# One written order for block 0, with scores set directly ahead of the preceding unit's outputs

## The chip, the core and the metric

The kernel runs on one core of a Trainium2 chip. The metric is the device time in microseconds (us) of one execution; the time of a kernel is the median over its runs. TensorE (PE) multiplies matrices into PSUM; VectorE (DVE), ScalarE (ACT) and GpSimd (POOL) do elementwise work; SyncE (SP) issues nearly all loads here. Each engine works through its own list of instructions in order and waits on semaphores for the others.

## What is computed

A linear-attention recurrence (RWKV) over 4 batches, 8 heads and 768 tokens of 48 channels, and after it a feed-forward layer on the 3072 tokens of 384 channels. The feed-forward weights come as 64-bit floats.

```python
for t in range(S):                                   # attention, per batch b and head h
    cur = einsum('bhd,bhe->bhde', u * k[:, :, t], v[:, :, t])
    y[:, :, t] = einsum('bhd,bhde->bhe', r[:, :, t], state + cur)
    state = w * state + einsum('bhd,bhe->bhde', k[:, :, t], v[:, :, t])
x = y.transpose(0, 2, 1, 3).reshape(B * S, H * D)    # 3072 x 384
h = x @ w_in                                         # 384 x 2048
g = where(h > 0, h, exp(min(h, 0)) - 1)
out = g @ w_out                                      # 2048 x 384
```

## The kernel before

The 768 tokens are cut into 6 blocks of 128. A **unit** is one block of one batch, written n.b: unit 1.2 is block 1 of batch 2. A block has 4 units, that is 512 tokens, and its feed-forward layer runs in 16 steps f, one for each 128 of the 2048 hidden channels.

**A unit's work.** `turn_in` (T) transposes r and k on TensorE; `decay_r` and `decay_k` (dr, dk, line L688) multiply them on VectorE by powers of w and their inverses; `scores` (A, L768) multiplies the two into two PSUM banks of scores; `take_scores` (pa, pb, L849) copies the scores under the mask over a diagonal that `diag_scores` wrote (Dp, Dq on GpSimd, Ep, Eq on ScalarE); `outputs` (Y) adds the state's part (`by_state`, L807 and L812), the scores' part (`by_keys`, L824) and, in the same call, makes the unit's contribution to the next state (`added_state`, L924); `split_x` (xh, xl) writes the result as a high and a low fp32r part; `new_state` (ns) updates the state; `key_rest` (kr, krd; L740) scales k for the state ahead of that. In block 0 there is no old state: `mask_scores` (m0, m1), `current_by_v` (vd, L859) and `first_outputs` (Y, L880 and L824) stand there, and S is `new_state`.

**A step of the layer.** `hidden` (hid f, L1031) is 9 matmuls of 512 columns, `project` (proj f, L1083) 9 more; between them stand `negative` (neg: two ScalarE passes, L1040 and L1041), `elu` (L1046, VectorE), and `split_g` (gh on ScalarE L1052, gl on VectorE L1054). `hidden` writes one of only two PSUM buffers named h, so hid f+2 can begin only when gl f has read the one of hid f.

**Weights.** They come once, during block 0, as pieces j: j = 2f is w_in's part f, j = 2f+1 is w_out's. Lw:j is the load (L212, L215). `widen` (wd, ScalarE L571), `merge` (ma, VectorE L580), `split_w` (sp; ScalarE L593 for w_in, GpSimd L591 for w_out) and `rest_w` (rs, rsd; VectorE L617, GpSimd or VectorE L615) make of a pair of 64-bit pieces two fp32r tables wh and wl, which stay in SBUF. The layer in block 0 therefore runs while its own weights are still coming.

**What sets the order.** Every engine gets its instructions in the order in which the program calls the helpers. Before block 0's layer that is the string START: words `name:unit`, called by `do`. Then comes BOTH for steps 0 to 2, and from step 3 on `step(n, f)` goes through the words of FIRST, the same ones at every step of block 0; a word such as A1 acts at the step that is one behind a unit's begin, and the units of block 1 begin at steps 2, 5, 8 and 11 (`BEGIN`). Blocks 1 to 5 go through LATER in the same manner. There, from unit 2.1 on, `insertion` (word AY) puts the scores of one unit directly ahead of the outputs of the unit before it: scores cut into 32-column pieces (L792) and then L807, L812, L824, L924, with one of the h buffers taken as an output buffer. In block 0 scores (L768) and outputs of block 1's units stand apart, each between matmuls of the layer.

Of the kernel before, what the change touches and what calls it, by code (L numbers as in the profile page):

```python
# [19 lines left out]
P = 128  # L20
# [16 lines left out]
EARLY = (0, 6)  # L37
# [16 lines left out]
proj krd1 swd2 Dp0 r3 rudx rudA-2 sumA-1 wd third tT+0
# [5 lines left out]
BEGIN = [2, 5, 8, 11]  # L60
# [6 lines left out]
class Kernel:  # L67
# [241 lines left out]
    def start(self):  # L309
# [3 lines left out]
        for b in (2, 3):  # L313
# [33 lines left out]
            "m1a": lambda b: self.mask_scores(0, b, 1, True),  # L347
            "vd": lambda b: self.current_by_v(0, b),
# [34 lines left out]
    def first_steps(self):  # L383
# [782 lines left out]
```

## Time and profile before

| | |
|---|---|
| median of 3 runs | 497.28 us (496.21 to 499.79) |
| the profiled execution | 496.31 us, its span 494.6 us |
| TensorE busy in the span | 485.3 us (98%) |
| VectorE, ScalarE, GpSimd busy | 304.2, 240.7, 107.3 us |
| busy from 25 to 110 us (block 0's layer): TensorE, VectorE, ScalarE | 84.09, 76.08, 58.15 of 85 us |
| loads | 49.11 MB in all; 184 GB/s over the first 25 us |

The span is from the first to the last instruction that the profile records; the rest of an execution lies around it. "Idle" of an engine is time between its instructions; a row gives it in brackets with the engine that ended it. Matmul rows overlap, so the cost of a group on TensorE is read here from starts: the start of the first matmul behind the group, less that of the last one ahead of it.

### The profile page before, as it was taken

Reading aid. Unit: us, or ns where it says so; the run is one execution under the profiler, and the core shown is the slowest. Engines: PE = TensorE matmul, PEld = TensorE weight load, DVE = VectorE, ACT = ScalarE, POOL = GpSimd, SP = SyncE. Lnnn points to the kernel's source line nnn. Section 1 sums busy time; section 2 is a strip of 40 time slices with the busy share of each in tenths; the row PEclk is TensorE's granted clock in tenths of the full one; section 3 lists DMA queues with packets and bytes.
Section 4 is the critical chain, followed back from the end, with each engine's and each line's share of the span. In section 5 each row is a group of like instructions: output and inputs, shape, how many; then the busy total and the mean of one; then the engine's idle time right before and its main releaser. Section 6 shows DMA issues by size and latency. Waiting matters only on the chain.

```text
span 494.6 us, 12125 instructions
## 1 busy us (share of the span) xinstructions
PE 485.3 (98%) x5013; PEld 403.4 (82%) x5013; DVE 304.2 (61%) x533; ACT 240.7 (49%) x458; POOL 107.3 (22%) x142
## 2 busy tenths in 40 slices
PE   8999999999999999999999999999999999999995
PEld 7787778787888888888888888888888888889995
DVE  7899988884686557657556575574674343433332
ACT  4377766734454444535435435445354453344341
POOL 7623332441132331221321321301011000000000
PEclk9999999999999999999999999999999999999999
DMA  9899987483364652544513625514343000010001
GB/s 142 223 231 204 213 197 190 94 153 89 84 139 105 135 121 43 130 118 72 121 52 84 151 67 108 142 44 92 101 79 100 11 1 2 8 33 20 5 0 69
DMA packets 108453, 49.11 MB, mean 99 GB/s; under 512 B 89442, under 2 KB 104292, under 8 KB 108388
## 3 DMA queue, kind: packets, MB, share of 16 engines
q1 hardware_dynamic: 96292, 43.52, 40.0%
q10 hardware_dynamic: 12096, 4.72, 4.0%
q8 instruction: 41, 0.67, 0.6%
q14 instruction: 24, 0.20, 0.1%
HBM read 35.12 MB, written 13.11 MB: 98 GB/s over the span
## 4 chain that ended last, share of the span: by engine, by line
PE 93%; DMA 3%; SPq 2%; DVE 1%; issue 0%; ACT 0%; DVEq 0%
PE ps_acc L1083 40%; PE ps_h L1031 39%; PE ps_y L824 4%; PE ps_a L792 4%; PE ps_y L812 1%; PE ps_y L924 1%; PE ps_a L768 1%; PE ps_y L807 1%; DMA raw<-in_k_dram 1%; DMA stage<-in_moe_w_out_dram 1%; DMA r_t<-in_r_dram 1%; SPq L169 1%; PE ps_y L880 1%; SPq L165 1%; PE ps_kT L628 0%; DMA w_col<-in_w_dram 0%
## 5 line engine op out<-in xcount | busy, mean ns | idle before, releaser
L1031 PE MATMUL ps_h<-x,wh 128*128 128x512 f32 (+1 forms) x582 | 192.6, 388 | 0.0
L1083 PE MATMUL ps_acc<-g,wh 128*128 128x512 f32 x480 | 164.6, 397 | 0.1
L1046 DVE SCALAR_TENSOR_TENSOR ps_h<-g,ps_h 128x512 f32<-128x512 f32 x96 | 66.6, 694 | 123.8 <-ACT g L1041 123.6
L1031 PEld LDWEIGHTS ps_h<-x,wh 128*128 128x128 f32 x582 | 108.8, 188 | 23.0 <-DVE g L1054 0.5
L1040 ACT ACTIVATE g<-ps_h 128x512 f32<-128x512 f32 x96 | 57.3, 596 | 123.2 <-PE ps_h L1031 95.0
L1031 PE MATMUL ps_h<-x,wl 128*128 128x512 f32 (+1 forms) x291 | 112.7, 387 | 0.0
L1083 PEld LDWEIGHTS ps_acc<-g,wh 128*128 128x128 f32 x480 | 90.0, 188 | 21.2 <-issue 0.8
L1054 DVE SCALAR_TENSOR_TENSOR g<-ps_h,g 128x512 fp32r<-128x512 f32 x96 | 66.3, 690 | 45.3 <-ACT g L1052 40.4
L1083 PE MATMUL ps_acc<-g,wl 128*128 128x512 f32 x240 | 93.6, 390 | 0.0
L1052 ACT ACTIVATE g<-ps_h 128x512 fp32r<-128x512 f32 x96 | 57.4, 598 | 72.7 <-DVE ps_h L1046 62.7
L1031 PEld LDWEIGHTS ps_h<-x,wl 128*128 128x128 f32 x291 | 54.7, 188 | 10.9
L1041 ACT ACTIVATE g<-g 128x512 f32<-128x512 f32 x96 | 60.7, 632 | 3.1
L842 POOL TENSOR_TENSOR a<-ident,diag 128x512 f32<-128x512 f32 x20 | 20.9, 1044 | 149.9 <-PE ps_y L924 81.2
L1083 PEld LDWEIGHTS ps_acc<-g,wl 128*128 128x128 f32 x240 | 45.1, 188 | 8.5
L676 POOL TENSOR_TENSOR tb<-rk,qw 128x512 f32<-128x512 f32 x16 | 20.7, 1297 | 70.3 <-DMA rk<-blocks 61.2
L1083 PE MATMUL ps_acc<-wh,g 128*128 128x384 f32 x128 | 33.8, 335 | 0.0
L849 DVE COPY_PREDICATED a<-mask,ps_a 128x512 f32<-128x512 int32 x40 | 29.3, 732 | 0.0
L838 ACT ACTIVATE a<-ident,diag 128x128 f32<-128x128 f32 x80 | 25.3, 391 | 0.0
L1083 PEld LDWEIGHTS ps_acc<-wh,g 128*128 128x128 f32 x128 | 23.2, 188 | 0.3
L571 ACT ACTIVATE wide<-stage 128x768 f16<-128x768 bf16 (+1 forms) x18 | 17.8, 991 | 9.9 <-DMA stage<-in_moe_w_in_dram 8.7
L949 ACT CAST x<-ps_y 128x256 fp32r<-128x256 f32 (+1 forms) x40 | 10.8, 324 | 22.8 <-DVE state L939 21.4
L1083 PE MATMUL ps_acc<-wl,g 128*128 128x384 f32 x64 | 21.4, 335 | 0.0
(114 smaller groups left out, 440.2 us busy)
## 6 DMA issues: line engine op xcount, KB each, us to landing
blocks<-tb SPq DMA_DIRECT2D x64, 128.0 KB, 2.3
rk<-blocks SPq DMA_DIRECT2D x16, 512.0 KB, 3.4
stage<-in_moe_w_out_dram SPq DMA_DIRECT2D x16, 383.8 KB, 5.4
stage<-in_moe_w_in_dram SPq DMA_DIRECT2D x64, 95.8 KB, 4.3
out_dram<-stage ACTq DMA_DIRECT2D x80, 48.0 KB, 1.7
r_t<-in_r_dram SPq DMA_DIRECT2D x17, 192.0 KB, 4.3
k_t<-in_k_dram SPq DMA_DIRECT2D x17, 192.0 KB, 4.9
v_t<-in_v_dram SPq DMA_DIRECT2D x17, 192.0 KB, 5.3
```

What stands on the lines that cost most here:

```text
L676: (self.nc.gpsimd if i else self.nc.vector).tensor_mul(dst, src, by)
L792: nc.tensor.matmul(un["pa"][i][keys, a * P : (a + 1) * P], lhsT=un["k"][rows, a, keys], rhs=un["r"][rows, a, :], start=True, stop=True, sk ...
L838: self.nc.scalar.activation(un["a"][i][:, a, :], self.ident, AF.Copy, scale=diag[:, a : a + 1])
L842: self.nc.gpsimd.tensor_mul(un["a"][i], self.ident.unsqueeze(1).to_broadcast([P, HP, P]), diag.unsqueeze(2).to_broadcast([P, HP, P]),)
L849: self.nc.vector.copy_predicated(un["a"][i], self.mask.bitcast(I32).unsqueeze(1).to_broadcast([P, HP, P]), un["pa"][i].rearrange("p (a t) ...
L1031: self.nc.tensor.matmul(ph[:, part], lhsT=a[:, c * P : (c + 1) * P], rhs=x[:, c, part], start=(c == 0 and i == 0), stop=(c == NC - 1 and i ...
L1040: nc.scalar.activation(g, ph, AF.Relu, scale=-1.0)
L1041: nc.scalar.activation(g, g, AF.Exp, scale=-1.0)
L1046: self.nc.vector.scalar_tensor_tensor(ph, g, -1.0, ph, op0=ALU.add, op1=ALU.max)
L1052: nc.scalar.activation(part, g, AF.Copy, scale=W_SCALE)
L1054: nc.vector.scalar_tensor_tensor(part, g, W_SCALE, self.g[n, f][2].bitcast(F32), op0=ALU.mult, op1=ALU.subtract)
L1083: self.nc.tensor.matmul(at, lhsT=lhs, rhs=rhs, start=(f == 0 and i == 0), stop=(f == NF - 1 and i == 2),)
```

## The change

START is rewritten, BOTH and FIRST are replaced by one string FIRST that writes out the whole of block 0 word by word, and `step` is left to blocks 1 to 5. A word with @ names a unit: `AY@1.1` is the new `inserted` for units 1.1 and 1.0, the same helper that `insertion` used. `BEGIN`, `stages`, `now` and the table of EARLY steps go. LATER and the tables of blocks 2 to 5 stay as they were. The conditions added to `by_keys`, `mask_scores` and `first_outputs` are for units without `vd`, of which the new strings have none; the words d0 to d1a are in no string.

```diff
+Lrk:2 pr jk:8 Tr:0 ub inv Lrk:3 dr:0 Tk:0 Lv:1 zw rua:0 rub:0 dk:0 PT Lw:0 Tr:1 Tk:1 dr:1 dk:1 rua:1 A:0 sum:0 rub:1
 ...
+rs:11 proj3 wd:7 elu5 Lw:17 ma:8 hid6 AY@1.1 gh5 Lw:18 ma:7 gl5 ru@1.1 sp:7 neg6 rsd:14 rs:13 sp:8 sum@1.1 elu6 Lw:20
+Lw:23 elu8 Lw:25 T@1.2 hid9 dr@1.2 ru@1.2 neg9 gh8 dk@1.2 Lw:26 sum@1.2 ma:11 gl8 sp:11 proj4 elu9 wd:12 AY@1.2 gh9
 ...
-        for op in BOTH.split():
-            if ":" in op:
+        units = self.unit_ops()
+        for op in FIRST.split():
+            if op == "third":
+                self.third_slot()
+            elif "@" in op:
+                name, at = op.split("@")
+                n, b = (int(i) for i in at.split("."))
+                self.done.add((name, n, b))
+                units[name](n, b)
+            elif ":" in op:
                 self.do(op)
             else:
-                layer[op[:-1]](int(op[-1]))
+                name = op.rstrip("0123456789")
+                layer[name](int(op[len(name):]))
 ...
+            "AY": lambda n, b: self.inserted((n, b), (n, b - 1)),
 ...
-        for at in range(3, NCH * NF):
+        for at in range(NF, NCH * NF):
             self.step(*divmod(at, NF))
 ...
+        self.inserted(new[0], old[0] if old else None)
+
+    def inserted(self, new, old):
+        nc, un = self.nc, self.units[new]
         un["pa"] = [self.bank("a") for _ in range(2)]
-        was = self.units[old[0]] if old else None
+        was = self.units[old] if old else None
```

Over the whole program the instruction counts change little. On TensorE 24 score matmuls of 128 columns become 96 of 32; the rest is the same set in another order. VectorE loses 5 scalings of k, 8 products for `ru`, 4 for `sw`, 4 state copies and one dr, and gains 3 `vd` and 4 `rest_w`; those that it loses go to GpSimd and ScalarE.

Three places show the order. The first is TensorE at the outputs of unit 1.0 (state_59 is the state of batch 0, wh_132 the w_in part of step 4 and the w_out part of step 3). Before, they stand alone behind hidden step 4:

```order
L1031 MATMUL ps_h<-x,wh_132 128x512
L807 MATMUL ps_y<-rk,state_59 32x128 x8
L812 MATMUL ps_y<-rk,state_59 32x128 x4
L824 MATMUL ps_y<-a,v_t_70 32x128 x16
L924 MATMUL ps_y<-v_t_70,k_t_69 32x48 x16
L1083 MATMUL ps_acc_664<-g_782,wh_132 128x512
```

Now they follow directly on the scores of unit 1.1, behind hidden step 6 (wh_136):

```order
L1029 MATMUL ps_h<-x,wh_136 128x512
L778 MATMUL ps_a<-rk 32x128 x32
L793 MATMUL ps_y<-rk,state_59 32x128 x8
L798 MATMUL ps_y<-rk,state_59 32x128 x4
L811 MATMUL ps_y<-a,v_t_70 32x128 x16
L922 MATMUL ps_y<-v_t_70,k_t_69 32x48 x16
L1081 MATMUL ps_acc_681<-g_961,wh_136 128x512
```

The outputs moved two steps later, and one place between the layer's matmuls became free; units 1.1 and 1.2 likewise join the scores of 1.2 and 1.3.

The second place is VectorE between the transposes and the scores of unit 1.2. Before, the two decays (L688) stand behind the layer's work of that step:

```order
L728 TENSOR_TENSOR ru<-ru,u_b 128x384
L939 TENSOR_TENSOR state_59<-sw,ps_y 48x4x48 x2
L580 SCALAR_TENSOR_TENSOR stage<-stage,wide 128x768
L733 TENSOR_REDUCE diag<-ru 128x8
L1046 SCALAR_TENSOR_TENSOR ps_h<-g,ps_h 128x512
L688 TENSOR_TENSOR rk<-ps_kT,qw 128x512
L1054 SCALAR_TENSOR_TENSOR g_938<-ps_h,g_936 128x512
L688 TENSOR_TENSOR rk<-ps_rT,pw 128x512
```

Now they stand next to each other and ahead of it:

```order
L1044 SCALAR_TENSOR_TENSOR ps_h<-g,ps_h 128x512
L671 TENSOR_TENSOR rk<-ps_rT,pw 128x512
L671 TENSOR_TENSOR rk<-ps_kT,qw 128x512
L716 TENSOR_REDUCE diag<-ru 128x8
L563 SCALAR_TENSOR_TENSOR stage<-stage,wide 128x768
L1052 SCALAR_TENSOR_TENSOR g_1130<-ps_h,g_1120 128x512
L1044 SCALAR_TENSOR_TENSOR ps_h<-g,ps_h 128x512
```

The merge of weights (L580, now L563), `gl` and `elu` moved behind the decays, and the two `ru` products left VectorE.

The third place is SP's list of loads in the prologue (raw is r, k or v of units 0.2 and 0.3). Before:

```order
L165 DMA raw<-in_r_dram 128x8x48
L165 DMA raw<-in_k_dram 128x8x48
L169 DMA v_t_73<-in_v_dram 128x8x48
L165 DMA raw<-in_r_dram 128x8x48
L165 DMA raw<-in_k_dram 128x8x48
L169 DMA raw<-in_v_dram 128x8x48
L212 DMA stage<-in_moe_w_in_dram 32x3x511 x4
L169 DMA raw<-in_v_dram 128x8x48
L212 DMA stage<-in_moe_w_in_dram 32x3x511 x4
L215 DMA stage<-in_moe_w_out_dram 128x1535
L212 DMA stage<-in_moe_w_in_dram 32x3x511 x4
L215 DMA stage<-in_moe_w_out_dram 128x1535 x2
```

Now:

```order
L171 DMA raw<-in_r_dram 128x8x48
L171 DMA raw<-in_k_dram 128x8x48
L171 DMA raw<-in_r_dram 128x8x48
L171 DMA raw<-in_k_dram 128x8x48
L175 DMA v_t_73<-in_v_dram 128x8x48
L218 DMA stage<-in_moe_w_in_dram 32x3x511 x4
L175 DMA raw<-in_v_dram 128x8x48
L218 DMA stage<-in_moe_w_in_dram 32x3x511 x4
L175 DMA raw<-in_v_dram 128x8x48
L221 DMA stage<-in_moe_w_out_dram 128x1535 x2
L218 DMA stage<-in_moe_w_in_dram 32x3x511 x4
```

The k of unit 0.3 moved ahead of the v of unit 0.1, the first two w_in pieces ahead of the v of 0.2 and 0.3, and the second w_out piece (j = 3) ahead of the third of w_in (j = 4).

## Rows read from the trace of the kernel before

**Rows 1.** Stages: stretch, length, busy time of each engine (instructions), clock, DMA share, GB/s.

```profile
0.00:25.00 25.00, 22.15 (x381) 18.72 (x381) 20.14 (x44) 9.64 (x16) 17.25 (x37) 1.00 0.90 184
25.00:110.00 85.00, 84.09 (x894) 67.92 (x896) 76.08 (x137) 58.15 (x107) 29.56 (x39) 1.00 0.86 185
```

**Rows 2.** TensorE's waits from 0 to 112 us: total us, times, longest.

```profile
PE ps_kT L628 <- DMA raw<-in_k_dram: 1.0, 1, 1.0
```

**Rows 3.** Timeline of TensorE (start, us, operation): scores of unit 1.0, standing alone.

```profile
39.30 0.39 PE L1031 MATMUL ps_h<-x,wl 128*128 128x512 f32 x1
39.52 0.39 PE L1031 MATMUL ps_h<-x,wh 128*128 128x512 f32 x1
39.84 1.16 PE L768 MATMUL ps_a<-rk 48*128 48x128 f32 x16
...
41.27 0.39 PE L1083 MATMUL ps_acc<-g,wl 128*128 128x512 f32 x1
```

**Rows 4.** Timeline of TensorE: outputs of unit 1.0, standing alone.

```profile
44.92 0.39 PE L1031 MATMUL ps_h<-x,wh 128*128 128x512 f32 x1
...
45.86 1.06 PE L824 MATMUL ps_y<-a,v_t 128*32 128x128 f32 x32
46.73 0.53 PE L924 MATMUL ps_y<-v_t,k_t 128*32 128x48 f32 x32
...
47.53 0.40 PE L1083 MATMUL ps_acc<-g,wl 128*128 128x512 f32 x1
```

**Rows 5.** Timeline of TensorE: scores of unit 2.2 with outputs of unit 2.1.

```profile
142.73 0.39 PE L1031 MATMUL ps_h<-x,wh 128*128 128x512 f32 x1
143.05 1.17 PE L792 MATMUL ps_a<-stage,tb 48*32 48x128 f32 x63
...
146.28 0.40 PE L1083 MATMUL ps_acc<-g,wl 128*128 128x512 f32 x1
```

**Rows 6.** Timeline of TensorE: outputs of unit 1.1, and scores of unit 1.2.

```profile
60.62 1.32 PE L824 MATMUL ps_y<-a,v_t 128*32 128x128 f32 x32
62.10 0.55 PE L924 MATMUL ps_y<-v_t,k_t 128*32 128x48 f32 x32 [0.16 <-DVE k_t L740]
...
71.57 0.39 PE L1031 MATMUL ps_h<-x,wh 128*128 128x512 f32 x1
72.61 1.16 PE L768 MATMUL ps_a<-rk 48*128 48x128 f32 x16 [0.65 <-DVE rk L688]
```

**Rows 7.** Timeline of VectorE: the two decays of unit 1.2.

```profile
70.42 0.68 DVE L688 TENSOR_TENSOR rk<-ps_kT,qw 128x512 f32<-128x512 f32 x1
...
71.78 0.68 DVE L688 TENSOR_TENSOR rk<-ps_rT,pw 128x512 f32<-128x512 f32 x1
```

**Rows 8.** Timeline of TensorE: first matmul of the layer; the three state products of block 0.

```profile
24.95 0.39 PE L1031 MATMUL ps_h<-x,wh 128*128 128x256 f32 x1
...
29.05 0.39 PE L1031 MATMUL ps_h<-x,wh 128*128 128x512 f32 x1
...
30.90 0.39 PE L1083 MATMUL ps_acc<-g,wl 128*128 128x512 f32 x1
```

**Rows 9.** Timeline of ScalarE: state copies, widenings that wait for weights, step 0's negative.

```profile
11.35 0.64 ACT L941 COPY state<-ps_st 48x192 f32<-48x192 f32 x2 [0.33 <-PE ps_st L924]
...
21.44 0.66 ACT L571 ACTIVATE wide<-stage 128x384 f16<-128x384 bf16 x1 [0.63 <-DMA stage<-in_moe_w_in_dram]
...
26.00 1.10 ACT L571 ACTIVATE wide<-stage 128x768 f16<-128x768 bf16 x1 [0.45 <-DMA stage<-in_moe_w_out_dram]
27.41 0.60 ACT L1040 ACTIVATE g<-ps_h 128x512 f32<-128x512 f32 x1 [0.31 <-PE ps_h L1031]
```

**Rows 10.** Timeline of VectorE: two operations of 128x384 in a row, and step 0's gl.

```profile
23.79 0.55 DVE L740 TENSOR_TENSOR raw<-raw,rev 128x384 f32<-128x384 f32 x1
24.26 0.55 DVE L901 TENSOR_TENSOR x<-ps_y,x 128x384 fp32r<-128x384 f32 x1
...
30.07 0.69 DVE L1054 SCALAR_TENSOR_TENSOR g<-ps_h,g 128x512 fp32r<-128x512 f32 x1 [0.66 <-ACT g L1052]
```

More of the change, by code (lines that the diff above doesn't have):

```diff
@@ L55 @@
+proj11 mb@2.0 rud@2.0 xh@1.3 rsd:30 gl12 elu13 ma:16 gh13 mr@2.0 rsd:28 hid15 sum@2.0 gl13 neg15 sw@1.3 sp:16 rs:27
+hid14 bk@2.0 rsd:29 proj12 ns@1.3 elu15 neg14 br@2.0 elu14 xl@1.3 gh15 v@1.3 gh14 proj13 third gl14 rk@1.3 gl15 rsd:31
+v@1.2
 """
@@ L409, in next_v @@
         self.load_v(1, b)
-    def stages(self, n, f):
-        return [(f - t, 1, b) for b, t in enumerate(BEGIN) if n == 0 and -1 <= f - t < 4]
     def units_at(self, times, step):
@@ L426, in third_slot, with unit_ops @@
         self.load_v(2, 1)
-    def step(self, n, f):
+    def unit_ops(self):
         nc = self.nc
-        k = f + 2 if n == 0 else NF + 1
-        units = self.stages(n, f)
-        last = divmod(n * NF + f - (1 if (n, f) < EARLY else 2), NF)
-        both = {
+        return {
             "ru": lambda n, b: self.current(n, b),
@@ L470, in step @@
         }
+    def step(self, n, f):
+        last = divmod(n * NF + f - 2, NF)
+        units = self.unit_ops()
         layer = {
-            "hid": lambda: self.hidden(n, f, self.rest_of(n, f)),
-            "ma": lambda: self.merge(k),
+            "hid": lambda: self.hidden(n, f),
             "neg": lambda: self.negative(n, f),
-            "sp": lambda: self.split_w(k),
-            "r4": lambda: self.rest_w(k, 1),
-            "r3": lambda: self.rest_w(k, 0),
-            "r4d": lambda: self.rest_w(k, 1, nc.vector),
-            "r3d": lambda: self.rest_w(k, 0, nc.vector),
             "elu": lambda: self.elu(n, f),
@@ L491, in step @@
         now = n * NF + f
-        for op in (LATER if n else FIRST).split():
+        for op in LATER.split():
             if op in layer:
@@ L495, in step @@
                 continue
[L496 to L506 removed]
+            name, times = op[:-3], {"A": SCORES, "Y": OUTPUTS, "T": TURNS}[op[-3]]
+            for m, b in self.units_at(times, now - int(op[-2:])):
+                if (name, m, b) not in self.done:
                     self.done.add((name, m, b))
[L508 removed]
+                    units[name](m, b)
     def warm(self, times):
@@ L821, in by_keys @@
             y, t = (un["py"][0], j * P) if len(un["py"]) == 1 else (un["py"][j // 2], j % 2 * P)
+            begins = n == 0 and (j != 1 if len(un["py"]) > 1 else j == 0 and "vd" not in un)
             for a in range(HP):
@@ L825, in by_keys @@
                     y[self.pair(a), t : t + P], lhsT=v[:, d : d + Q], rhs=un["a"][i][:, a, :],
-                    start=(n == 0 and j != 1 and len(un["py"]) > 1), stop=bool(last), skip_group_check=True,
+                    start=begins, stop=bool(last), skip_group_check=True,
                 )
```

91 lines of the change are left out of this document (37 added, 54 removed).

## The prediction

> **What bounds the kernel now.** I read the page first, then the stages, then TensorE's waits, and last the timeline around each place that the change touches. In block 0's layer TensorE is busy 84.09 of 85 us, VectorE 76.08 and ScalarE 58.15 [rows 1]: TensorE sets the time and VectorE is close behind it. Before 25 us TensorE is busy 22.15 us, at 184 GB/s of loads [rows 1]. The clock is granted in full in both stages [rows 1], so no term below comes from it. Blocks 1 to 5 keep their order. A gain can thus come from three things only: TensorE work that the new order saves, waits of TensorE that it removes, and an earlier start of the layer. All of them lie in the first 110 us, and the waits there are small: the longest is one of 1.0 us for the k of unit 0.3 in the prologue [rows 2].
>
> **The joined scores and outputs.** I read costs as start to start, from the layer's last matmul ahead of a group to the second one behind it (the first is lengthened by the switch); that holds two ordinary spacings of about 0.22 us (39.30 to 39.52 [rows 3]). Scores alone: 41.27 − 39.52 = 1.75, less 0.45, makes 1.30 us [rows 3]. Outputs alone: 47.53 − 44.92 = 2.61, makes 2.16 us [rows 4]. Joined: 146.28 − 142.73 = 3.55, makes 3.10 us [rows 5]. So a join saves 1.30 + 2.16 − 3.10 = 0.36 us, and three of them **−1.1 us**. The scores themselves are not cheaper: cut small they take 1.17 us, whole 1.16 [rows 3, 5]. The saving is one place less at which the stream of 512-column matmuls is interrupted. The rows of blocks 1 to 5 show this same form, so I give it little spread: −0.9 to −1.2.
>
> **The two waits in block 0.** The scores of unit 1.2 begin 72.61 − 71.57 = 1.04 us after the matmul ahead of them, where unit 1.0 needed 39.84 − 39.52 = 0.32 [rows 3, 6]: 0.72 lost. VectorE is the cause: its second decay of that unit begins at 71.78, 1.36 us after the first, with a `gl` between [rows 7]. The new list has both decays in a row behind the transposes, ahead of merge and `gl`; between transposes and scores stand 18 matmuls of the layer as before, some 4 us, and two decays need 2 × 0.68 = 1.4 [rows 7]. The outputs of unit 1.1 lose 62.10 − 60.62 = 1.48 against 46.73 − 45.86 = 0.87, that is 0.61 us, on late scores and on the scaled k [rows 4, 6]. In the new order they stand several layer groups further back, and k is scaled by GpSimd long before. Together **−1.3 us**; bounds 0 (both waits come back elsewhere) and −1.3.
>
> **The start of the layer.** It begins at 24.95 [rows 8]. What it waits for in the new order: `vd` of units 0.1 to 0.3 is on VectorE, not on GpSimd, and that of 0.3 needs its v. That v is now issued behind w_in's second piece. All loads ahead of it are then those which before ended with that piece, and the piece was there at 21.4, where ScalarE stopped waiting [rows 9]. The loads run at the rate of the queue throughout, so I let v land at 21.4. Behind it VectorE's list has, up to the last thing that the first hidden matmuls need: `vd`, one low part of x, a mask of scores, a merge, a rest of weights. Four of these are 128x384, at 0.47 us from start to start [rows 10], the mask is 128x512 like a decay, 0.68 [rows 7]: 2.6 us, so the layer begins at 24.0, **−1.0 us**. Bounds: if v lands when VectorE first reaches it, about 1 us sooner, −2.0; if it lands 1 us later, 0. The wait for the k of unit 0.3 [rows 2] goes too, since its load is one earlier, but that is inside the −1.0.
>
> **The ramp.** Before, the three state products of units 0.1 to 0.3 cost 30.90 − 29.05 − 0.45 = 1.4 us in one place [rows 8]. Now one stands in the middle of hidden step 0, one behind it, one next to transposes: one interrupted place more, at the 0.36 of the join, **+0.4 us** (0.2 to 0.6). Then hidden step 2 needs `gl` of step 0. Its chain begins on ScalarE, whose list has a widening ahead that waits for weights until 26.00 and takes 1.10 [rows 9], and the same loads as before stand ahead of those weights. Two state copies follow, 0.64 [rows 9]: step 0's `negative` begins at 27.75, where it began at 27.41. From there to the end of `gl` it was 30.07 + 0.69 − 27.41 = 3.35 us [rows 9, 10]; two more copies stand in it, about half of them in ScalarE's slack, so 31.4. TensorE gets there at 24.0 + 4.3 (hidden 0 and 1, from 24.95 to 29.28 [rows 8]) + 1.3 (two state products at 0.67) + 1.35 (transposes and the third) = 30.95. That is a new wait of **+0.45 us** (0 to 1.5).
>
> **Covered edits, and what I can't see.** The rest of the moved work is off TensorE. VectorE sheds some 6 us net (22 operations less 7 gained, most of them 0.47 from start to start [rows 10]), and GpSimd takes most of it, where 29.56 of 85 us were busy [rows 1]; its results (scaled k, `ru`) are needed several microseconds later. If that cover fails, a late scaled k costs what unit 1.1 shows, about 0.6. Weights are asked for in another order, hidden steps run one step further ahead of projections, and the loads of unit 1.3 follow the second join with three layer groups (6 us) to land. Somewhere in 85 us of a new order a wait will appear; I take **+0.6 us**, one wait like the two removed; bounds 0 and 2.6 (twice both).
>
> **The sum.** −1.1 − 1.3 − 1.0 + 0.4 + 0.45 + 0.6 = −1.95 us, against this execution's 496.31: 494.4. The median of the runs shown is 497.28, 1.0 above it; I take half of that difference, **494.8 us**.
>
> **Rivals.**
> - *All gains, no new wait* (chance 0.15): v lands early, hidden step 2 finds its buffer: −1.1 − 1.3 − 2.0 + 0.4 = −4.0, so 492.8 with the half difference. For it: VectorE is relieved. Against it: ScalarE's widening cannot start before 26.0.
> - *The waits only move* (0.17): VectorE is the same engine at 76 of 85 us, and what was late for scores is late for `gl`, on which hidden steps wait. Only the joins remain, less the ramp: −1.1 + 0.4 + 0.45 = −0.25, so 496.6 with the half difference.
> - *Slower, by the order of the loads* (0.16): ScalarE works in order, and the widening of pair 2 stands ahead of step 0's `negative`. If its weights land later than 26.0, `gl`, hidden step 2 and all behind it shift one to one. From 1.95 us later, at 28.0, the whole gain is gone; at 30.0 the sum is −1.95 + 4.0, so 498.9 with the half difference. For it: loads of 0.90 and 0.86 share in these stages [rows 1] have no reserve. Against it: the set of loads ahead is the same.
> - *Small matmuls cost more* (0.02): 96 score matmuls instead of 24 each bring a fixed cost. If each of the 144 more rows in the trace (a matmul shows as two) cost what a row takes there, 1.17/63 = 0.02 us [rows 5], the joins lose 2.9 on top of the sum: 497.7 with the half difference. Rows 5 against rows 3 show no such cost. [...]
>
> **How the numbers follow.** My forecast has 0.50; its own range is 493.6 to 496.1. The 8-in-10 range takes in the first two rivals and half of the third: 492.4 to 498.0. Faster by over 1% (about what a measurement of this kernel can tell from no change) means under 492.3: the end of the first rival, 0.06. Slower by over 1%, over 502.3, needs the third at twice its size: 0.03. Within 1%: 0.91.
>
> **What would show it.** Right: the joined groups of 1.1 to 1.3 at 3.1 us; no wait on L688 or the scaled k ahead of them; first hidden matmul near 24.0; a wait of some tenths ahead of hidden step 2, ended by `gl` on VectorE; all of block 1's rows shifted by about 2 us. Wrong: `vd` of unit 0.3 starting far from 21.4; a wait of ScalarE's widening past 26.0; TensorE waits of over 1 us in block 0, above all at the transposes of unit 1.3 for loads.

## The result, and the profile after

The changed kernel takes 502.2 us (median of 15 runs, 499.88 to 507.33), the kernel before 497.11 (median of 15, 495.73 to 499.79). The ratio is 1.010, with a 95% interval of 1.008 to 1.012. The forecast was 494.8 us, 2.3 us below the median of before; the kernel came out 5.1 us above it.

| | before | after |
|---|---|---|
| profiled execution: time (span), us | 496.31 (494.6) | 501.82 (500.0) |
| first hidden matmul | 24.95 [rows 8] | 25.51 |
| first scores of block 1 | 109.14 | 114.22 |
| from there to the end of the span | 385.5 | 385.8 |

Nearly the whole difference, 5.1 us of the 5.4 by which the span grew, arises before 114 us. The two stages answer to [rows 1]: span of the stage, busy time of each engine (x instructions), granted clock, DMA share, GB/s.

```profile
0.00:25.00 25.00, 21.59 (x370) 18.51 (x374) 21.41 (x44) 9.47 (x16) 18.36 (x37) 1.00 0.98 185
25.00:110.00 85.00, 80.08 (x980) 64.68 (x969) 71.58 (x116) 58.00 (x112) 44.50 (x50) 1.00 0.77 178
```

From 25 to 110 us TensorE is busy 80.08 instead of 84.09, and GpSimd 44.50 instead of 29.56. The clock is granted in full in both stages (1.00), so it plays no part. TensorE's waits up to 118 us (total, times, longest):

```profile
PE ps_h L1029 <- DVE g L1052: 1.9, 3, 1.4
PE ps_y L922 <- issue: 1.7, 1, 1.7
...
PE ps_y L793 <- DVE g L1052: 1.3, 1, 1.3
```

L1029 is the hidden matmul, L793 and L922 are parts of a join, and `g L1052` is `gl`, which gives a buffer of the hidden matmuls back. By the rule of the prediction (start to start, two ordinary spacings off), the 5.1 us come from: start of the layer +0.56; state products +0.31 (0.46 + 0.57 + 0.67 where [rows 8] had 1.39); scores of unit 1.0 +0.32 (0.26 of it is a wait of hidden step 3, right behind them, for `gl1`); transposes of unit 1.2 +0.18; hidden step 7 +0.37; hidden step 11 +1.59; and the six groups that became three joins +1.30 (4.65 + 5.33 + 3.14 = 13.12, where before scores of 1.1 to 1.3 and outputs of 1.0 to 1.2 cost 11.82 together). That makes 4.63; 0.45 lie in small spacings. Only the third join costs what was forecast. Of the other two, and of hidden step 11, the timelines follow.

**The join of unit 1.1.** TensorE, then ScalarE, then VectorE (start, duration, [idle before <- what ended it]):

```profile
53.81 1.16 PE L778 MATMUL ps_a<-rk 48*32 48x128 f32 x64
56.31 0.45 PE L793 MATMUL ps_y<-rk,state 48*32 48x128 f32 x16 [1.34 <-DVE g L1052]
```

```profile
49.84 0.60 ACT L1038 ACTIVATE g<-ps_h 128x512 f32<-128x512 f32 x1 [0.53 <-PE ps_h L1029]
...
52.56 2.10 ACT L554 ACTIVATE wide<-stage 128x768 f16<-128x768 bf16 x2 [1.46 <-DMA stage<-in_moe_w_in_dram]
54.50 0.59 ACT L1050 ACTIVATE g<-ps_h 128x512 fp32r<-128x512 f32 x1
```

```profile
51.33 0.68 DVE L1044 SCALAR_TENSOR_TENSOR ps_h<-g,ps_h 128x512 f32<-128x512 f32 x1
53.74 1.91 DVE L563 SCALAR_TENSOR_TENSOR stage<-stage,wide 128x768 int32<-128x768 int32 x2 [1.73 <-DMA stage<-in_moe_w_in_dram]
55.57 0.68 DVE L1052 SCALAR_TENSOR_TENSOR g<-ps_h,g 128x512 fp32r<-128x512 f32 x1
```

A join puts one part of its outputs (`ps_y`, tag "h") into one of the two buffers of the hidden matmuls; outputs standing alone use two banks of another tag. So the joins bring the users of those two buffers in block 0 from 16 to 19. The buffer is that of hidden step 5, and comes back with `gl5`. `elu5` is done at 52.0, and `gh5` could follow. But ScalarE's list has two widenings ahead of it, and the first waits 1.46 us for weights; VectorE's list has the merges of the same two pairs ahead of `gl5`. From `negative` to the end of `gl` it takes 56.25 − 49.84 = 6.4 us, where step 0 took 3.35 [rows 9, 10].

**The join of unit 1.2 and hidden step 11.**

```profile
75.08 0.50 PE L922 MATMUL ps_y<-v_t,k_t 128*32 128x48 f32 x26
77.26 0.29 PE L922 MATMUL ps_y<-v_t,k_t 128*32 128x48 f32 x6 [1.68 <-issue]
...
81.25 0.47 PE L1029 MATMUL ps_h<-x,wh 128*128 128x512 f32 x1 [1.43 <-DVE g L1052]
```

```profile
77.17 1.08 ACT L554 ACTIVATE wide<-stage 128x768 f16<-128x768 bf16 x1 [2.18 <-DMA stage<-in_moe_w_in_dram]
78.12 1.25 ACT L825 ACTIVATE a<-ident,diag 128x128 f32<-128x128 f32 x4
79.28 0.51 ACT L947 CAST x<-ps_y 128x256 fp32r<-128x256 f32 x2
```

```profile
79.66 0.73 DVE L937 TENSOR_TENSOR state<-sw,ps_y 48x192 f32<-48x192 f32 x2 [3.71 <-ACT x L947]
80.41 0.69 DVE L1052 SCALAR_TENSOR_TENSOR g<-ps_h,g 128x512 fp32r<-128x512 f32 x1
```

TensorE stops in the middle of 32 equal matmuls and waits for nothing that the profile names. Then hidden step 11 waits for `gl9`, which stands on VectorE behind the new state of unit 1.1, which waits for the high part of x on ScalarE, which stands behind the widening of pair 13, which waits 2.18 us for weights. VectorE is idle for 3.71 us, although `gh9` stands ahead of that widening on ScalarE and `gl9` could have followed it.

### The profile page after: what moved, and what is told of

Same layout as the page of the kernel before. It is cut to its first block, busy times and chain, and to the rows that moved or that the text cites. A ratio compares the mean times of both kernels' runs of the same rounds, so it can differ in the third digit from the quotient of the medians.

```text
span 500.0 us, 12416 instructions
## 1 busy us (share of the span) xinstructions
PE 485.8 (97%) x5157; PEld 404.0 (81%) x5157; DVE 305.2 (61%) x518; ACT 241.8 (48%) x467; POOL 122.6 (25%) x152
## 4 chain that ended last, share of the span: by engine, by line
PE 85%; DVE 5%; DMA 3%; SPq 2%; ACT 2%; issue 1%; DVEq 0%; ACTq 0%
PE ps_acc L1081 38%; PE ps_h L1029 37%; PE ps_a L778 4%; PE ps_y L811 3%; PE ps_y L798 1%; DMA stage<-in_moe_w_in_dram 1%; SPq L218 1%; DVE stage L563 1%; PE ps_y L922 1%; PE ps_y L793 1%; DMA stage<-in_moe_w_out_dram 1%; SPq L171 1%; DVE g L1052 1%; ACT wide L554 1%; DMA r_t<-in_r_dram 1%
## 5 line engine op out<-in xcount | busy, mean ns | idle before, releaser
L1029 PE MATMUL ps_h<-x,wh 128*128 128x512 f32 (+1 forms) x582 | 193.3, 389 | 1.9 <-DVE g L1052 1.9
L1029 PEld LDWEIGHTS ps_h<-x,wh 128*128 128x128 f32 x582 | 109.0, 188 | 25.9 <-ACT a L825 1.8
L1029 PE MATMUL ps_h<-x,wl 128*128 128x512 f32 (+1 forms) x291 | 112.8, 388 | 0.0
L1052 DVE SCALAR_TENSOR_TENSOR g<-ps_h,g 128x512 fp32r<-128x512 f32 x96 | 66.1, 690 | 41.3 <-ACT g L1050 37.3
L1029 PEld LDWEIGHTS ps_h<-x,wl 128*128 128x128 f32 x291 | 54.7, 188 | 10.7
L825 ACT ACTIVATE a<-ident,diag 128x128 f32<-128x128 f32 x84 | 26.7, 392 | 0.0
L1081 PE MATMUL ps_acc<-wl,g 128*128 128x384 f32 x64 | 21.4, 335 | 0.0
```

The source lines that it names most:

```text
L825: self.nc.scalar.activation(un["a"][i][:, a, :], self.ident, AF.Copy, scale=diag[:, a : a + 1])
L1029: self.nc.tensor.matmul(ph[:, part], lhsT=a[:, c * P : (c + 1) * P], rhs=x[:, c, part], start=(c == 0 and i == 0), stop=(c == NC - 1 and i ...
L1052: nc.vector.scalar_tensor_tensor(part, g, W_SCALE, self.g[n, f][2].bitcast(F32), op0=ALU.mult, op1=ALU.subtract)
L1081: self.nc.tensor.matmul(at, lhsT=lhs, rhs=rhs, start=(f == 0 and i == 0), stop=(f == NF - 1 and i == 2),)
```

## Experiments: the losses one by one, on the kernel after

Times are also given as a ratio to the kernel before on the same chip, with a 95% interval; after itself is 1.010 (1.008 to 1.012). Among the repairs below only the last, of all losses together, has an interval clear of that one; what each single repair did is read from its rows. The rows are those of one execution, and places that an edit didn't touch vary too. The theories that the expectations name: 1, the lists (chains that free buffers stand behind weights); 2, the gap is a wait for instructions; 3, VectorE is slowed by GpSimd beside it. From the joins alone on they are joined by A, the new order of layer and weights is at fault and the joins are sound; B, the joins themselves; C, the prologue; and D, the ring of the two hidden buffers, in which a join is one user more.

**The layer's chains ahead of the weights.**

```diff
-... neg5 wd:8 dk@1.1 rs:11 proj3 wd:7 elu5 Lw:17 ma:8 hid6 AY@1.1 gh5 Lw:18 ma:7 gl5 ...
+... neg5 dk@1.1 rs:11 proj3 elu5 Lw:17 hid6 AY@1.1 gh5 Lw:18 gl5 wd:8 wd:7 ma:8 ma:7 ...
-... AY@1.2 gh9 v@1.0 rsd:22 Lw:28 wd:13 proj8 ma:12 hid11 Ep@1.2 xh@1.1 hid10 ns@1.1 Eq@1.2 rk@1.1 rs:21 Lw:27 T@1.3 gl9 ...
+... AY@1.2 gh9 gl9 v@1.0 rsd:22 Lw:28 proj8 ma:12 hid11 xh@1.1 Ep@1.2 hid10 ns@1.1 Eq@1.2 wd:13 rk@1.1 rs:21 Lw:27 T@1.3 ...
```

> The kernel after the change, but each layer chain before the weights: `gh5` and `gl5` stand ahead of the widenings and merges of pairs 8 and 7, and `gl9`, the high part of x and the new state of unit 1.1 ahead of the widening of pair 13. Theory 1 (lists in order: `gl5` and `gl9` are late because ScalarE and VectorE wait for weights ahead of them; the join of unit 1.1 and hidden step 11 wait for the buffer that these free): TensorE's waits on `gl` at the join of unit 1.1 (1.34 us) and at hidden step 11 (1.43 us) shrink below 0.4 us, and the time falls by 2 to 3 us, to about 499.5. Rival A (the weights themselves are late, and TensorE needs them soon behind): the waits on `gl` go, but hidden steps 7, 8 and 13 wait for pairs 7, 8 and 13 instead, time 502 as after. [...]

Measured: 501.28 us, 1.0085 (1.0067 to 1.0103). The join of unit 1.1 costs 3.07 us, clean; hidden step 11 starts without a wait. But:

```profile
62.44 0.50 PE L1026 MATMUL ps_h<-x,wh 128*128 128x512 f32 x1 [1.55 <-DVE g L1049]
...
84.70 0.47 PE L1026 MATMUL ps_h<-x,wh 128*128 128x512 f32 x1 [1.64 <-DVE x L946]
```

Hidden step 7 now waits for `gl6` (the widenings stand ahead of `gh6` instead of `gh5`), and hidden step 10 for the join's own buffer, which the low part of x frees. The waits are owed to the lists, as theory 1 says, but they moved on by one user of the buffers. Rival A named the right kind of outcome and the wrong cause: neither of them waits for its weights. This execution also lost some 2 us at hidden steps 2 and 3, ahead of everything edited, where after lost 0.26.

**Thirty-two tiny matmuls more at the start.**

```diff
+        for _ in range(32):
+            self.nc.tensor.matmul(junk[0:Q, 0:1], lhsT=self.ident[:, 0:Q], rhs=self.ident[:, 0:1], start=True, stop=True)
```

> The kernel after the change with 32 tiny matmuls (128 columns of weights, one column moved) more in the warming at the start, before any data has landed. They change nothing behind them but the number of TensorE instructions ahead of each place. Theory 2 (the gap of 1.68 us in the middle of the join of unit 1.2, which ends on nothing that the profile shows, is a wait for the instructions themselves, at a fixed place of the instruction stream): the gap leaves `added_state` of unit 1.2, appears some other number of instructions away or not at all, and the time moves by up to 1.7 us either way. Rival (the gap belongs to the work of that place: a buffer or the outputs' operands): it stays inside the outputs of unit 1.2's join, 1.5 to 1.8 us, and the time is 502 as after, give or take 0.5.

Measured: 504.58 us, 1.0184 (1.0136 to 1.0231). The time says nothing here, since the added matmuls held up the prologue (the layer starts at 28.94, 3.43 later, with a granted clock of 0.74 from 8 to 12 us). The place does: the join of unit 1.2 runs through, 3.58 us, and no gap of that kind over 0.2 us is left in block 0.

```profile
76.36 1.06 PE L815 MATMUL ps_y<-a,v_t 128*32 128x128 f32 x32
77.23 0.52 PE L926 MATMUL ps_y<-v_t,k_t 128*32 128x48 f32 x32
```

I counted the matmul records ahead of the gap in the join of unit 1.2 in every kernel that has it: 976 in after and in e1, e3, e5, e8 and e9, 975 in e11, 977 in e7, in three different orders of the work. In all but e11 that is also the same work, behind 26 or 27 of the 32 equal matmuls; in e11 the join begins 9 records later, and the gap comes behind 16 of the 32. So it keeps to the place in the stream and not to the work. The count alone doesn't make it, though: in e2 the 976th record lies in the same join, 82 records into it, and nothing waits there. What differs is when the instruction queue (q8 in the profile: 42 packets, 0.69 MB in after) starts its packet of 16 KB. In the eight kernels with the gap it starts while TensorE is already in the join, between its 903rd and its 962nd record, and TensorE goes on 2.4 to 3.0 us after that start; the gap is shortest (0.64 us, e11) where the packet starts at the 903rd, longest (2.56, e8) at the 962nd. In after the packet starts at 74.47 us and takes 1.26, and the gap lasts from 75.58 to 77.26. In e2 the packet starts at 66.64, 9.5 us ahead of the 976th record. So the gap goes with a packet of instructions that starts late inside a join, a place of 152 rows of matmuls and as many of weight loads in 3 us; the profile itself names no releaser.

**Decayed v back on GpSimd in the prologue.**

```diff
-... S:0 vdd:1 dk:3 Y:1 ... vdd:2 m0:2 m1:2 A:3 vdd:3 xl:1 ...
+... S:0 vd:1 dk:3 Y:1 ... vd:2 m0:2 m1:2 A:3 vd:3 xl:1 ...
```

> The kernel after the change, with the decayed v of units 0.1 to 0.3 back on GpSimd in the prologue, as before. Theory 3 (VectorE's multiplications that read two tiles of SBUF run as long as an operation of GpSimd beside them: 1.28, 0.91 and 1.49 us instead of 0.55): VectorE's excess in the first 25 us falls from 1.8 us to under 1, the first hidden matmul comes at 25.0 or earlier, and the time falls by about 0.5 to 501.7. Rival (GpSimd's own `vd` is slower and late for the state products): the state products or hidden step 2 come later, and the time rises by 0.5 or more, to over 502.5.

Measured: 503.81 us, 1.0154 (1.0137 to 1.0170): the rival. TensorE waits 3.3 us for GpSimd's `vd`, and then runs at half its clock for 4 us (granted clock is the third column from the right):

```profile
18.00:20.00 2.00, 0.17 (x17) 0.03 (x4) 1.53 (x1) 0.82 (x3) 2.00 (x3) 1.00 0.97 196
20.00:22.00 2.00, 0.53 (x12) 0.50 (x16) 0.55 (x2) 0.00 (x0) 2.00 (x3) 0.65 0.96 334
22.00:24.00 2.00, 2.00 (x44) 1.85 (x40) 1.20 (x2) 0.00 (x0) 1.03 (x2) 0.50 1.16 246
```

The layer starts at 30.19, 4.7 us later than in after. In this prologue `vd` is better on VectorE, slowed as it is there.

**The joins of units 1.1 and 1.2 undone.**

```diff
-hid5 Lw:16 ... hid6 AY@1.1 ... hid9 dr@1.2 ru@1.2 ... AY@1.2
+hid5 Y@1.0 Lw:16 ... hid6 A@1.1 ... hid9 dr@1.2 Y@1.1 ru@1.2 ... A@1.2
```

> The kernel after the change with the joins of units 1.1 and 1.2 undone: the outputs of unit 1.0 stand alone behind hidden step 5 and those of unit 1.1 behind hidden step 9, the scores of units 1.1 and 1.2 alone where the joins stood; that of unit 1.3 stays a join. Theory 1 (a join takes one of the two buffers of the hidden matmuls, so it waits for `gl` of the step before): the outputs alone take the same buffer two steps earlier, where it is free; the 1.34 us go, each undone join costs 0.36 back, and the time falls by 1 to 3 us, to 499 to 501. Rival (the waits are owed to late weights, wherever the outputs stand): hidden steps 7 and 11 wait on `gl` as long as the joins did, and the time is 502 to 503.

Measured: 501.82 us, 1.0102 (1.0085 to 1.0119), within neither theory. The waits on `gl` at the joins and the 1.6 us of hidden step 11 are gone (hidden step 8 loses 0.7), as theory 1 says. Its reason for the outputs is wrong, though: standing alone they take two banks of another tag, not an earlier turn at the same buffer. And new waits replace the old: the outputs of unit 1.1 wait 1.23 us, and the transposes of unit 1.3 1.2 us for r and k.

```profile
PE ps_y L793 <- DVE rk L671: 1.2, 1, 1.2
PE ps_h L1029 <- DVE g L1052: 1.0, 2, 0.6
PE ps_kT L611 <- DMA k_t<-in_k_dram: 0.7, 1, 0.7
PE ps_rT L611 <- DMA r_t<-in_r_dram: 0.5, 1, 0.5
```

**The moved operations back on VectorE** (scaled k, `ru`, decayed state of block 0: `kr`, `ru`, `sw` become `krd`, `rud`, `swd`).

> The kernel after the change, with the scaled k, the decayed k and the decayed state of block 0 (kr:2, and kr, ru, sw of units 1.0 to 1.3 and 2.0 where they stand) back on VectorE. Theory 3 (VectorE's operations run as long as GpSimd's beside them: 6.07 us too long in 14 operations from 25 to 110 us): VectorE's excess falls below 2 us, TensorE's waits on `gl` (1.3 and 1.4 us) shrink, time 498 to 500.5. Theory A (the loss lies in the order of layer and weights): VectorE gets 9 more operations of 0.5 to 0.7 us, the waits on `gl` stay or grow, time 502 or more.

Measured: 504.40 us, 1.0133 (1.0092 to 1.0173): theory A. GpSimd falls to 25.29 us of 85 (44.50 in after), TensorE's waits for VectorE grow (2.5 us on `gl` for hidden steps, 1.7 in joins), and the gap in the join of unit 1.2, at the same place, is 2.56 us long. VectorE's operations are still 4.6 us too long in sum (6.07 in after): it is less the number of operations on GpSimd that lengthens them than which of them meet. How much of the 5.1 us that is worth stays open.

**One projection ahead of the join.**

```diff
-hid6 AY@1.1 gh5 ... sp:11 proj4 elu9 ... hid12 proj7 gh10
+hid6 proj4 AY@1.1 gh5 ... sp:11 proj7 elu9 ... hid12 gh10
```

> The kernel after the change with two projections placed elsewhere: that of step 4 ahead of the join of unit 1.1 (it stood behind hidden step 9), that of step 7 in its place (it stood behind hidden step 12). TensorE then has 2.5 us of other work between hidden step 6 and the join, while `gl5` runs. Theory D: the wait of 1.34 us inside the join of unit 1.1 goes, also the 0.37 behind it, and comes back nowhere in full: time 500 to 501. Rival (the whole row of waits is one late chain of weights): the waits at the join go, but hidden step 11 waits as much longer, or the join of unit 1.2: time 502 to 503.

Measured: 500.00 us, 1.0086 (1.0055 to 1.0116); the interval overlaps that of after. In the rows it is theory D: the join of unit 1.1 costs 3.10 us, hidden step 7 has no wait, and hidden step 11 waits 0.51 us instead of 1.43, not longer. It isn't free, since there is one projection less behind hidden step 12, and hidden steps 15 and 14 now wait:

```profile
101.63 0.50 PE L1029 MATMUL ps_h<-x,wh 128*128 128x512 f32 x1 [0.91 <-DVE g L1052]
104.22 0.50 PE L1029 MATMUL ps_h<-x,wh 128*128 128x512 f32 x1 [0.24 <-DVE g L1052]
```

**Whole scores in block 0's joins**, 16 rows of matmuls instead of 64.

```diff
-            for keys in (self.pair(q) for q in range(P // Q)):
+            for keys in [slice(0, P)] if new[0] == 1 else [self.pair(q) for q in range(P // Q)]:
```

> The kernel after the change with the scores of block 0's three joins whole (16 matmuls of 128 columns of weights) instead of cut in four (64): a join then has 104 matmuls instead of 152, and as many weight loads. Theory 2 (the gap of 1.68 us inside the join of unit 1.2 is a wait for instructions: it has come at the same place of the stream, behind the same number of TensorE's matmuls, in four kernels of different orders, and was gone when 32 more stood ahead): no gap that ends on nothing the profile shows, over 0.3 us, inside any join; the scores themselves take as long; time 500 to 501. Rival (cut scores are cheaper or the gap belongs to the outputs): joins 0.3 us dearer or the gap stays, time 502 to 503.

Measured: 501.90 us, 1.0107 (1.0074 to 1.0140).

```profile
75.29 0.52 PE L922 MATMUL ps_y<-v_t,k_t 128*32 128x48 f32 x32
...
80.82 0.47 PE L1029 MATMUL ps_h<-x,wh 128*128 128x512 f32 x1 [2.72 <-DVE g L1052]
```

The 32 matmuls run through and the join costs 3.57 us instead of 5.33: theory 2 on the gap. The packet of instructions starts inside this join too, at 75.42 us, but the 976th record comes only at 89.90, and no gap there either. Nothing is won, against its time: hidden step 11 starts at 80.82, as it did at 81.25, and waits as much longer. Its date is set by ScalarE and VectorE, so the gap lay in the shadow of that wait.

**Gap and step 11 together, then all three.**

```diff
-AY@1.2 gh9 v@1.0 rsd:22 Lw:28 wd:13 proj8 ma:12 hid11 Ep@1.2 xh@1.1 hid10 ns@1.1 Eq@1.2 ... T@1.3 gl9 ... krd@1.2 xl@1.1
+AY@1.2 gh9 gl9 v@1.0 rsd:22 Lw:28 xh@1.1 proj8 ns@1.1 xl@1.1 ma:12 hid11 Ep@1.2 wd:13 hid10 Eq@1.2 ... T@1.3 ... krd@1.2
```

> The kernel after the change with whole scores in block 0's joins and, besides, what hidden steps 11 and 10 wait for moved ahead of the widening of pair 13: `gl9` behind `gh9`, and the high part of x, the new state and the low part of x of unit 1.1 directly behind it. The projections stay where the change put them. Theory D (each of the three losses is its own late release of a buffer of the hidden matmuls, with the gap for instructions as the fourth): the 1.6 us of hidden step 11 go and come back at most to a third at hidden step 10 or 12, the gap is gone, the wait of 0.95 to 1.34 at the join of unit 1.1 stays; first scores of block 1 near 111.5 (after: 114.22), time 499 to 500. Rival A (weights set the pace, all waits move on to pair 13): hidden step 12 or 10 waits as long as step 11 did, time 501.5 or more.

> All repairs together on the kernel after the change: the projection of step 4 ahead of the join of unit 1.1 (that of step 7 in its place), whole scores in block 0's joins, and `gl9` with the parts of x and the state of unit 1.1 ahead of the widening of pair 13. Theory D: the named losses add up (1.9 at the join of 1.1 and behind it, 1.7 gap, 1.6 at hidden step 11, 5.2 together), less 1 to 1.5 for a new wait near hidden step 13, as it came when the projection of step 7 was moved: time 497 to 499, no longer distinguishable from before or up to 0.4% above it. If the time stays over 500, the losses named aren't the whole of it.

Measured: 500.26 us, 1.0065 (1.0042 to 1.0089), and with the projection moved as well 499.60, 1.0057 (1.0039 to 1.0076). TensorE's waits from 25 to 118 us, first of e13, then of e14:

```profile
PE ps_y L792 <- DVE g L1051: 1.9, 2, 1.6
PE ps_h L1028 <- DVE g L1051: 0.2, 1, 0.2
```

```profile
PE ps_h L1028 <- DVE g L1051: 1.9, 3, 0.9
PE ps_y L792 <- DVE g L1051: 0.3, 1, 0.3
```

In e13 the join of unit 1.1 waits, 1.61 us, and no other place over 0.3, as theory D says (first scores of block 1 at 111.62). In e14 three joins cost 3.24, 3.57 and 3.25 us, less than the 11.82 of before. The repairs bring back 2.6 us of the 5.1 by the medians, 2.1 by the ratios, where 3.7 to 4.2 were expected, and the time misses the expected 497 to 499: 0.72 stood at hidden step 3, a wait for `gl1` in a place that no repair touched, and 1.5 at hidden steps 15 and 14, as in e11. Another 1.1 us belongs to the prologue, next.

## Experiments: parts of the change on the order of before

Block 0 of before was written out in the list of after (the same instructions in the same order on each engine), and one part of the change put into it.

**The prologue alone.**

> The kernel before with another part of the change alone: the new prologue (its order of loads, decayed v on VectorE, state product of unit 0.1 in it), and behind it block 0 in the order of before. Theory A (the loss lies in the layer's new order): the first hidden matmul at about 25.5 as after, the layer as long as before (84.2 us from the first hidden matmul to the first scores of block 1), time 496.5 to 498. Theory C (the prologue issues the weights of pairs 2 and 3 later, and the whole layer runs behind them): the layer takes 86 us or more, waits of TensorE on `gl` or weights between 30 and 80 us, time 499 to 501.

Measured: 498.07 us, 1.0025 (1.0012 to 1.0038): theory A, at the upper end of its range. The first hidden matmul comes at 25.17, the first scores of block 1 at 109.83, 84.7 us behind it. The new prologue costs 1.1 us (0.6 to 1.9 by the interval) instead of giving 1.0.

**The joins alone.** The edit, for unit 1.1, as it stands in the last of three runs:

```diff
-hid4 ... Y@1.0 ... xh@1.0 xl@1.0 ... rk@1.0 v@1.0 hid5 ns@1.0 ... Dp@1.1 ... Eq@1.1 hid6 A@1.1 ... pa@1.1
+hid6 AY@1.1 rk@1.0 v@1.0 ... ns@1.0 gh6 gl6 xh@1.0 xl@1.0 Dp@1.1 ... Eq@1.1 hid7 pa@1.1
```

> The kernel before, its whole order of block 0 written out, with one part of the change alone: the outputs of units 1.0, 1.1 and 1.2 are moved back by two layer steps to stand behind the cut scores of the next unit (three joins), and what hangs on them (masks, parts of x, state, loads) with them. Prologue, order of weights, lead of hidden steps over projections and the division between VectorE and GpSimd stay as before. Theory A (the loss of the change lies in the order of the layer and its weights, the joins themselves are sound): the three joins cost 3.1 to 3.5 us each, no wait on `gl` of over 0.3 us, the first scores of block 1 at 107 to 108.5 (before 109.14), time 494.5 to 496.5. Theory B (the joins bring the loss, by the buffer of the hidden matmuls that they take or by the instructions that they add): waits of 1.3 to 1.7 us inside joins here too, time 498 to 500.

> Both parts together: the new prologue and the three joins, with the layer, its weights and the division between the engines in the order of before. Theory A: time 494.5 to 497.5, all of the loss of the change (5 us) gone, since what is left out is only the layer's new order. Theories B or C: 499 or more. If prologue and joins each cost nothing alone and together 2 us or more, the cause is an interaction of the two.

In these two, the first runs, `rk@1.0` stood ahead of the join, so k of unit 1.2 came over the scaled k of 1.0 that the join still reads, which changes the state and the outputs of block 1. Measured: 508.38 us, 1.0224 (1.0199 to 1.0249), and with the prologue 508.81, 1.0233 (1.0209 to 1.0257). TensorE waited for those loads, so they tell nothing about the joins, but this: moving outputs back also moves back the loads of the unit after next.

```profile
112.36 0.87 PE L922 MATMUL ps_y<-v_t,k_t 128*32 128x48 f32 x32 [4.82 <-DMA k_t<-in_k_dram]
```

With the loads behind the join:

> The joins alone once more, on the order of before: the outputs of units 1.0 to 1.2 stand behind the cut scores of the next unit. Here the loads of r and k that overwrite the scaled k stand behind the join that reads it (in the earlier run of the joins alone they stood ahead of it, which changed the values of block 1's outputs and made two joins wait for those loads: 4.8 us in one). Theory D (the ring of the two buffers of the hidden matmuls: a join takes one of them as 17th to 19th user, and a buffer comes back only after a chain of 5 to 6 us on ScalarE and VectorE, which weights share in block 0): waits of 0.5 to 2 us at joins or at the hidden steps behind them in this order too, time 498 to 501. Theory A (only the new order of layer and weights is at fault, joins are sound): joins at 3.1 to 3.5 us, time 494.5 to 496.5.

Measured: 505.73 us, 1.0173 (1.0146 to 1.0201), outside both ranges. Of it 4.28 us come from this list and not from the change: the blocks of unit 2.0 had to be turned one step later, and its scores waited for them. Without these it would be about 501.4. The three joins cost 5.78 (with hidden step 7), 5.37 and 4.33 us, 15.5 together against 11.82 apart. So they are not sound in this order, against theory A. But the wait that theory D names is there only once, the 1.60 us of hidden step 7; 3.2 us are waits for a decay, which no theory named, and 0.7 the gap that ends on `issue`:

```profile
55.91 1.13 PE L778 MATMUL ps_a<-rk 48*32 48x128 f32 x63 [0.94 <-DVE rk L671]
...
60.48 0.50 PE L1029 MATMUL ps_h<-x,wh 128*128 128x512 f32 x1 [1.60 <-DVE g L1052]
```

Every join waits about 1 us for a decay, where the scores of units 1.1 and 1.3 alone had no wait in before. Without outputs in between, TensorE reaches the scores 2 us earlier, and VectorE doesn't.

**The two waits alone.**

```diff
-dk@1.2 gh8 gl8 dr@1.2
+dk@1.2 dr@1.2 gh8 gl8
-krd@1.1
+kr@1.1
```

> The kernel before with only the two waits of block 0 taken on: both decays of units 1.1 to 1.3 in a row on VectorE, ahead of `gh` and `gl` of that step, and the scaled k of unit 1.1 on GpSimd. The prediction's step: the scores of unit 1.2 lose 0.72 us less and the outputs of unit 1.1 0.61 less, 496.9 minus 1.3, about 495.6. Rival (the waits move to the hidden matmuls, since `gl` stands one decay later): the scores of 1.2 cost 1.3 us, and a hidden step behind waits 0.3 to 0.7 on `gl`; 496.5 to 497.5.

Measured: 496.53 us, 0.9988 (0.9971 to 1.0004), not told apart from before. In the rows the step is right: the scores of unit 1.2 cost 1.29 us (2.01 before) and the outputs of unit 1.1 2.37 (2.79), 1.1 together, and no hidden step behind waits. (This execution has another wait, of 1.80 us at 32.33, for weights ahead of the first projection; it lies ahead of all that was edited, and the granted clock fell to 0.58 from 32 to 36 us.) From the start of hidden step 2 to the first scores of block 1 it takes 75.15 us, 76.41 in before: the gain isn't taken back there.

```profile
73.22 0.68 DVE L671 TENSOR_TENSOR rk<-ps_kT,qw 128x512 f32<-128x512 f32 x1
73.82 0.68 DVE L671 TENSOR_TENSOR rk<-ps_rT,pw 128x512 f32<-128x512 f32 x1
```

```profile
74.45 0.39 PE L1029 MATMUL ps_h<-x,wh 128*128 128x512 f32 x1
74.77 1.16 PE L751 MATMUL ps_a<-rk 48*128 48x128 f32 x16
```

This is the lowest median of all kernels here, though not by more than the measurement's uncertainty. None beats before by a margin that can be told.

## Why the prediction was wrong, step by step

- **The joins, −1.1: right in the form, wrong in the place.** A join that has what it needs costs 3.14 us (the third in after) and 3.10 (e11), forecast 3.10. The step that failed is the sentence behind it: "The rows of blocks 1 to 5 show this same form, so I give it little spread". They show the form without the work of block 0 around it. In block 0 the chain that frees a buffer took 6.4 us instead of 3.35, and the join is one more user of that buffer. It is moreover a place where TensorE goes through 304 rows (152 matmuls, 152 weight loads) in 3 us, and in that of unit 1.2 it stood for 1.68 us beside a packet of instructions that began only within the join. The three joins cost 1.3 us more than the six groups, instead of 2.4 less (joins and two waits). Without the waits the form does gain: the three joins of e14 cost 10.1 us together.
- **The two waits, −1.3: right in the rows** (e10: −1.1; its time can't be told from before), but the joins stood in their place with 1.34 and 1.68 us.
- **The start of the layer, −1.0: wrong in sign.** The layer started at 25.51, not 24.0; in ten executions with this prologue it started between 24.81 and 26.45, in four with the old one between 24.09 and 25.23. The load order did better than forecast: v of unit 0.3 landed at 20.1, not 21.4. VectorE did worse, and reached its `vd` only at 22.04:

```profile
16.88 1.28 DVE L846 TENSOR_TENSOR vd<-v_t,diag 128x384 f32<-128x384 f32 x1
...
20.01 0.91 DVE L846 TENSOR_TENSOR vd<-raw,diag 128x384 f32<-128x384 f32 x1
...
22.04 1.49 DVE L846 TENSOR_TENSOR vd<-raw,diag 128x384 f32<-128x384 f32 x1
```

```profile
16.75 1.00 POOL L711 TENSOR_TENSOR ru<-ru,u_b 128x384 f32<-128x384 f32 x1
17.71 1.50 POOL L669 TENSOR_TENSOR rk<-rk,pw 128x512 f32<-128x512 f32 x1
19.18 1.33 POOL L723 TENSOR_TENSOR raw<-raw,rev 128x384 f32<-128x384 f32 x1
21.83 1.29 POOL L669 TENSOR_TENSOR a<-a,mask 128x512 f32<-128x512 f32 x1 [1.33 <-ACT a L668]
```

  The three took 3.7 us, not 3 × 0.47. Each began while an operation of GpSimd was running and ended 0.41 us behind that one's end (17.75, 20.51, 23.12). The term was sized with rows that had no GpSimd operation beside them [rows 10].
- **The ramp, +0.85: the state products right** (+0.31, forecast +0.4); the wait of hidden step 2, +0.45, wasn't there in this execution, though 0.46, 0.51 and 1.22 us stood there in e1, e11 and e8. Hidden step 3, which the prediction doesn't treat, waited for `gl1` instead: 0.26 here, 0.6 to 0.7 in e4, e11 and e14, 1.62 in e1, nothing in e2, e3, e8, e12 and e13.
- **Unseen waits, +0.6 with bounds 0 to 2.6: mis-sized most.** 1.34 + 0.37 + 1.68 + 1.59 = 5.0 us. I had no mechanism for them and so gave the size of one wait of before. It could have been seen that the list puts widenings and merges ahead of `gh5`, `gl5` and `gl9`, and that the joins take the buffers which these free.
- **The rivals.** "Slower, by the order of the loads" had the mechanism, ScalarE in order behind a widening that waits for weights, for pair 2; it happened at pairs 8 and 13 instead, each time ahead of a buffer that TensorE needed next, and in a small way at pair 3: its widening, ahead of step 1's `negative`, waited 1.06 us for weights in after and 2.31 in e1. "Small matmuls cost more" fell as a price for each matmul: 64 cut ones took 1.16, 1.23 and 1.17 us in after's three joins, 16 whole ones 1.16 (e12). What went with their number is the gap: 1.68 us in the join of unit 1.2 in after, none there in e12.

What stays open: 0.45 us of the 5.1 that lie in small spacings; what the longer operations of VectorE (below) are worth in block 0; and part of the loss as time: the repairs that took the waits at the joins and at hidden step 11 away got back 2.1 to 2.6 us of the 5.1, the prologue alone costs 1.1, and the rest went into waits elsewhere. What makes a packet of instructions start as late as in the join of unit 1.2 is open too.

## What to carry to other kernels

A group of instructions whose price is read where the other engines are idle is no price for a place where they are busy: ask which buffer it takes, who frees that buffer, and what stands ahead of that on its engine's list. Put work that waits for a load behind the chain that gives TensorE its buffers back, not ahead. And repair such waits together: two of them in one chain hide each other, and taking away one alone (the gap, e12) gave nothing.

## What the runs showed of the hardware

**VectorE beside GpSimd.** Lines of VectorE from 25 to 110 us (busy, mean ns of one), of after and, in the last fence, of before:

```profile
L600 DVE SCALAR_TENSOR_TENSOR wl<-stage,wh 128x384 fp32r<-128x384 f32 x16 | 11.3, 705 | 0.2
...
L1052 DVE SCALAR_TENSOR_TENSOR g<-ps_h,g 128x512 fp32r<-128x512 f32 x14 | 9.6, 682 | 0.1
```

```profile
L617 DVE SCALAR_TENSOR_TENSOR wl<-stage,wh 128x384 fp32r<-128x384 f32 x15 | 8.2, 546 | 0.0
```

The rest of the weights, with both inputs in SBUF, takes 705 ns instead of 546; `gl`, with one input in PSUM, 682 as before (690). Sorted by what GpSimd did at the time, the 11 of L600 beside an operation of GpSimd took 0.78 us in the mean and up to 1.37, those alone 0.55. What counts is which began first. Five began while a two-input operation of GpSimd was running: they took 0.68 to 1.37, and each ended some 0.4 us behind the end of that operation, like the three `vd` above. The other six, where GpSimd began later or ran a cast, took 0.54 to 0.57. The operations `elu`, `gl`, decays and masks, which read PSUM, took as long either way: begun while a two-input operation of GpSimd was running 0.68 to 0.72, 0.68, 0.68 to 0.69 and 0.74 to 0.75 us, alone 0.67 to 0.70, 0.68 to 0.69, 0.68 to 0.69 and 0.73 to 0.74. In before, all 15 of L617 stood alone.

**A gap beside a late packet of instructions.** Eight kernels lost 0.6 to 2.6 us at one place of TensorE's stream, and TensorE went on 2.4 to 3.0 us behind the start of a packet of instructions that began late in the join of unit 1.2. Where the packet began 9.5 us or more ahead of the 976th record, with 32 matmuls more ahead (e2) or fewer in block 0's joins (e12 to e14), nothing is left there.

**Clock.** In e3 TensorE had waited 3.3 us, and its granted clock then stood at 0.50 from 22 to 26 us: the layer started 4.7 us later than in after. In e10 the wait of 1.80 us at 32.33 was followed by a granted clock of 0.58 from 32 to 36 us.
